# Attention and mixer on one core: tails of two pairs together, more seven-product parts, another order of loads

## The chip, the core and the metric

The kernel runs on one core of a Trainium2 chip. Its engines run side by side, each with its own queue of instructions: TensorE (PE; its weight loads are listed apart as PEld), VectorE (DVE), ScalarE (ACT), GpSimd (POOL) and SyncE (SP). POOL and SP issue most of the DMA transfers. The metric is the time of one execution in microseconds (us) on the device, the median of several runs.

## The reference

Sliding-window attention with a linear bias (window 128, 8 heads of 64), and on its output a mixer: a two-layer product over the 576 tokens, added to its input, then a two-layer product over the 512 channels with 1536 hidden units, added again.

```python
batch, n_heads, seq, head_dim = (8, 8, 576, 64)
mask = (rel >= 0) & (rel < window)
scores = np.where(mask, scale * q @ k.T + bias, -1e9)
attn = softmax(scores); x = attn @ v            # heads side by side: (8, 576, 512)
h = np.maximum(xt @ w_tok1, 0.0) @ w_tok2       # xt: x with tokens and channels exchanged
u = x + h.transpose(0, 2, 1)
h2 = np.maximum(u @ w_ch1, 0.0) @ w_ch2         # 512 -> 1536 -> 512
return u + h2
```

## The kernel before

**Tiling.** The 576 tokens of a batch are four blocks of 128 and 64 left over. Two batches make a pair; the 64 + 64 left-over rows of a pair share one block of 128 rows, the tail (`TAIL`, block 8 of a pair). Matrices are bf16, sums are float32 in PSUM, which has eight banks of 512 float32 columns.

**Stages.** For batch b, `side(b)` does the attention and the token mix, `main(b)` the channel mix. `side(b + 1)` is interleaved with `main(b)`, so that the matmuls of the one fill the gaps of the other. Batch 7's `main` has no other batch beside it.

- `scores`: for each block, `q k^T` of the 128 keys before it and of its own (L693), two instructions for the even and the odd heads after that (`Exp` on ACT, L716; the mask on DVE, L726). The first block of a batch has keys of its own kind only, yet its scores lie spread in four banks, as those of the others.
- `values`: the product with v (L760), the reciprocal and the scaling (L773, L776).
- `token_mix`: the first product over the tokens (L805 for the four blocks, L815 for the 64 rows of the tail), a ReLU, the second product (L848, L844 for the tail), and the addition of x (L866). From batch 1 on, the tail's 64 rows are copied to the other half of the partitions (`xt`, L800), so that two 64-row matmuls can run side by side in L815. The result is transposed by DMAs from SP (L874; from batch 2 on).
- `main`: twelve chunks of the first channel product, each of 4 matmuls of 512 columns (L1045) and a ReLU (L1051 on ACT, L1052 on DVE). Where `UNITS[b]` is not zero, the last units of four chunks are computed with seven half-size products instead of eight (`unit`, L967, 28 matmuls of 256 columns), with four differences of the input first (`halves`, L931), copies out (L982), additions (L991) and ReLUs (L993, L995). In the kernel before only batch 7 does this, with three units.
- `second`: the second channel product for the four blocks, with seven products instead of eight (L1240), sums before it (L1070) and evictions (L1203) in the order `PRODUCTS`. The last one of batch 7 is `last_product` (L1269, L1273).
- The tail of a pair belongs to the odd batch: three `tail_piece`s of 16 matmuls of 128 columns (L1088, ReLU L1093), then 12 matmuls of 512 columns for the second product (L1133, eviction L1140, stores L1150).

**The order.** `Plan` collects all these operations with a cost and a rank and works out, before anything is emitted, in which order each engine's queue gets them; buffers come from rings (`ps` for the banks, `ob` for six output buffers, `r2` for two hidden buffers and so on). `SEEDS` shifts the ranks a little by pseudo-random amounts, and some constants (`CASTS`, `LATE`, `TURN`, `RATES`, `EV`) are the planner's due times and rates. Where the plan has PE idle early, `spin` puts in matmuls on zeros (L1325). The loads are issued by POOL in the order of the string `LOADS`: q, k, v with the number of a block; W1, W2 and P1, T0 are the weights of the token mix and their left-over rows; A0 to A3 and B0 to B3 are quarters of the two channel weights (`WC1`, `WC2`).

```python
LOADS = ("k1 q1 k2 q2 v0 k8 q8 v1 v2 v8 v3 W1 q7 q4 k4 W2 q6 "
         "k6 A0 k7 q5 A3 k5 v7 v4 A1 v6 v5 A2 B0 T0 P1 B2 B1 B3")
```

q and k of blocks 0 and 3 come by SP and ACT ahead of these, as float32.

Of the kernel before, what the change touches and what calls it, by code (L numbers as in the profile page):

```python
# [73 lines left out]
class Plan:  # L74
# [235 lines left out]
    def emit(self, spin):  # L310
# [11 lines left out]
        for _, _, go in sorted(work, key=lambda w: w[:2]):  # L322
# [13 lines left out]
PADT = False  # L336
# [9 lines left out]
SEEDS = {0: 846071, 4: 412855, 5: 343328, 6: 901394, 7: 671959, 8: 764867, 10: 416701, 11: 351752, 12: 70309, 20: 619675, 21: 120696, 22: 577973, 23: 405716, 30: 213057, 31: 165847, 32: 71954, 40: 404590, 41: 482568, 50: 286568, 51: 611926, 60: 579527, 61: 819459, 62: 379002, 70: 640395, 71: 934419, 72: 439456, 80: 109511, 81: 910233, 82: 748762, 90: 519950, 91: 197367, 101: 150347, 102: 405724, 110: 7956, 111: 36992, 112: 363882, 120: 129293, 122: 874736, 130: 359970, 131: 803027, 140: 23914, 141: 388902, 142: 496852, 150: 220523, 151: 220010, 152: 75231, 153: 900190}  # L346
# [3 lines left out]
EV = 0.0  # L350
# [6 lines left out]
HALVED = 2  # L357
BANKS = 8
ALIKE = 0
UNITS = [0, 0, 0, 0, 0, 0, 0, 3]  # L360
# [6 lines left out]
CASTS = [5000.0, 5680.0, 7560.0, 8040.0]  # L367
PACKET = 0.813
LATE = (2400.0, 3500.0)
FETCH = 9000.0  # L370
STORE = 774.0
TURN = [(792.0, 1267.0), (1380.0, 2400.0)]
RATES = [(0.37, 0.23), (0.52, 0.35), (0.47, 0.18)]
# [4 lines left out]
LOADS = ("k1 q1 k2 q2 v0 k8 q8 v1 v2 v8 v3 W1 q7 q4 k4 W2 q6 "  # L378
         "k6 A0 k7 q5 A3 k5 v7 v4 A1 v6 v5 A2 B0 T0 P1 B2 B1 B3")
# [3 lines left out]
def kernel(  # L383
# [45 lines left out]
              lambda s: ps[:, s[0] : s[1] + 1, :].rearrange("p a b -> p (a b)"))  # L429
    ONE, TWO = [(4,), (5,), (6,), (7,)], [(0, 1), (2, 3)]  # L430
    TWICE = [(4, 5), (6, 7)]
# [9 lines left out]
    ring("v", AHEAD, [P, H, 2 * D])  # L441
# [4 lines left out]
    ring("ub", 2, [P, NB, DM])  # L446
# [4 lines left out]
    ring("uTt", 1, [P, NCB, P])  # L451
    ring("r2", 2, [P, NHT, NC * P])
    ring("r2t", 1, [P, NHT, P])
# [53 lines left out]
    for t in plan.rings["v"].slots:  # L507
        dve_.memset(t[:, :, D : D + 1], 1.0)

# [118 lines left out]
    qkT, xbs, ubs, r1s, uts, wides = {}, {}, {}, {}, {}, []  # L628
    turned, marks, turns = {}, {}, {}
# [41 lines left out]
    def scores(pr, blk, half, rank, behind=()):  # L671
# [5 lines left out]
        sp = [bank(TWO + THIRD if first else TWO) for _ in range(2)]  # L677
# [8 lines left out]
        def wide(e):  # L686
            return sp[e]().rearrange("p (i k c) -> p i k c", i=4, k=2)

        def go():
            for i in range(4):  # L690
                for kind, kb, a, z in work:
                    for e in range(2):
                        pe_.matmul(wide(e)[:, i, kind, a:z],  # L693
                                   lhsT=ts[kb]()[e * D : (e + 1) * D, NHP + i, :],
                                   rhs=ts[blk]()[e * D : (e + 1) * D, i, a:z], start=not slanted, stop=True,
                                   skip_group_check=slanted)
# [15 lines left out]

        one = pr >= MERGEM
# [20 lines left out]
    def values(pr, blk, half, pb, rank):  # L734
# [12 lines left out]
        for es in ([[0, 1]] if both else [[0], [1]]):  # L747
# [3 lines left out]
            def view(ot=ot, n=n):  # L751
                v = ot().rearrange("p (e c) -> p e c", e=n)[:, :, 0 : 4 * (D + 1)]
                return v.rearrange("p e (i d) -> p e i d", i=4)
# [35 lines left out]
    def token_mix(b, rank):  # L789
# [4 lines left out]
        pad = PADT and b > 0  # L794
# [33 lines left out]
        uTt = plan.buf("uTt") if half else None  # L828
# [3 lines left out]
        for blk in blocks:  # L832
# [29 lines left out]
            if fold:  # L862
                plan.op("ACT", 600, lambda blk=blk, ht=ht, hs=hs: act_.copy(out=ub()[:, blk, :], in_=ht()[:, hs]),
                        rk, part=(ub, blk), uses=[ht])
            else:
                plan.op("DVE", 690, lambda blk=blk, ht=ht, hs=hs: dve_.tensor_tensor(  # L866
                    out=ub()[:, blk, :], in0=ht()[:, hs], in1=xb()[:, blk, :], op=ALU.add), rk,
                    part=(ub, blk), uses=[ht], reads=tks)
        for blk in blocks:
            if b >= FROM_U:  # L870
                def turn(blk=blk):
                    c = blk % NC
                    to = uTt()[:, :, :] if blk == TAIL else uT()[:, :, c * P : (c + 1) * P]
                    nc.sync.dma_start_transpose(out=to, in_=ub()[:, blk, :])  # L874

                turned.setdefault(b, []).append(plan.op(
                    "SP", 1200, turn, rank(0), part=(uTt if blk == TAIL else uT, blk), reads=[(ub, blk)], bus=1000))
                continue
            ut = bank()

            def go(blk=blk, ut=ut):
                for cb in range(NCB):
                    pe_.transpose(ut().bitcast(BF16)[:, cb * P : (cb + 1) * P],
                                  ub()[:, blk, cb * P : (cb + 1) * P], ident[:, :])

            def copy(blk=blk, ut=ut, eng=dve_.tensor_copy):
                c = blk % NC
                to = uTt()[:, :, :] if blk == TAIL else uT()[:, :, c * P : (c + 1) * P]
                eng(out=to, in_=ut().bitcast(BF16)[:, 0 : NCB * P].rearrange("p (a b) -> p a b", a=NCB))

            rk = rank(224)
            plan.op("PE", 224, go, rk, makes=ut, reads=[(ub, blk)])
            plan.op("DVE", 425, copy, rk, part=(uTt if blk == TAIL else uT, blk), uses=[ut],
                    other=("ACT", 600, lambda copy=copy: copy(eng=act_.copy)))
        uts[b] = (uT, uTt, blocks)
# [23 lines left out]
    def halves(b, rank, uT):  # L919
# [4 lines left out]
        blks = [x for x in uts[b][2] if x != TAIL]  # L924
# [92 lines left out]
    def main(b, rank):  # L1017
        pr, half = b // 2, b % 2
        uT, uTt, blocks = uts[b]
        ub = ubs[pr]  # L1020
        r2 = plan.buf("r2")
        r2t = plan.buf("r2t") if half else None
# [58 lines left out]
        def tail_piece(t):  # L1081
            cx = bank()

            def gox(t=t, cx=cx):
                for i in range(4):
                    for cb in range(NCB):
                        tt = t - 3 + i
                        pe_.matmul(cx()[:, i * P : (i + 1) * P], lhsT=WC1[:, cb, tt * P : (tt + 1) * P],  # L1088
                                   rhs=uTt()[:, cb, :], start=cb == 0, stop=cb == NCB - 1)

            rk = rank(900)
            plan.op("PE", 896, gox, rk, makes=cx, reads=[(uTt, TAIL)], needs=[lc1[t]])
            plan.op("ACT", 600, lambda t=t, cx=cx: act_.activation(  # L1093
                out=r2t()[:, t - 3 : t + 1, :], in_=cx().rearrange("p (a b) -> p a b", a=4), func=ACT.Relu),
                rk, part=(r2t, t // 4), uses=[cx])

        if not UNITS[b]:
            turn_ = [0, 1, 2, 6, 7, 8, 3, 4, 5, 9, 10, 11] if quick else list(range(NHT))
            for at, t in enumerate(turn_):
# [3 lines left out]
                if half and at % 4 == 3:  # L1103
                    tail_piece(at)
        else:
            tt = halves(b, rank, uT)
            for u in range(NHT // 4):
# [7 lines left out]
                if half:  # L1115
                    tail_piece(4 * u + 3)
        if b == B - 1 and not quick:
            blocks = blocks[:2] + [TAIL] + blocks[2:4]
        if quick:
            second(b, rank, r2, ss, sums, ub)  # L1120
            blocks = [TAIL] if half else []
        for blk in blocks:
            cuts = [slice(0, DM)]
            if b == B - 1 and blk == blocks[-1]:
                cuts = [slice(0, DM // 2), slice(DM // 2, DM)]
            for cols in cuts:
                o2 = bank()
                n = cols.stop - cols.start
                for g in range(NHT // 3):
                    def go(blk=blk, g=g, o2=o2, cols=cols):  # L1130
                        for t in range(3 * g, 3 * g + 3):
                            l = r2t()[:, t, :] if blk == TAIL else r2()[:, t, (blk % NC) * P : (blk % NC + 1) * P]
                            pe_.matmul(o2()[:, cols], lhsT=l, rhs=WC2[:, t, cols], start=t == 0, stop=t == NHT - 1)  # L1133

                    rk = rank(648)
                    rd = [(r2t, g * 3 // 4), (r2t, (g * 3 + 2) // 4)] if blk == TAIL else [(r2, t) for t in range(3 * g, 3 * g + 3)]
                    plan.op("PE", 649 * n / DM, go, rk, reads=rd, needs=lc2[3 * g : 3 * g + 3],
                            **({"makes": o2} if g == 0 else {"adds": o2}))
                ob = plan.buf("ob")
                plan.op("DVE", 160 + 530 * n / DM, lambda blk=blk, o2=o2, ob=ob, cols=cols: dve_.tensor_tensor(  # L1140
                    out=ob()[:, cols], in0=o2()[:, cols], in1=ub()[:, blk, cols], op=ALU.add), rk, makes=ob, uses=[o2],
                    reads=[(ub, blk)])

                late = b >= FROM_P and blk not in blocks[-2:] or FROM_P <= b < B - 1
                q_ = nc.gpsimd if late else nc.sync

                def store(blk=blk, ob=ob, cols=cols, q_=q_):
                    if blk == TAIL:
                        for i in range(2):
                            (nc.scalar if i and b == B - 1 else q_).dma_start(  # L1150
                                out=out[2 * pr + i, NC * P : S, cols], in_=ob()[i * R : (i + 1) * R, cols])
                    else:
                        q_.dma_start(out=out[b, (blk % NC) * P : (blk % NC + 1) * P, cols], in_=ob()[:, cols])

                if late:
                    plan.dma(store, P, -1, uses=ob)
# [204 lines left out]
```

## Time and profile before

| | |
|---|---|
| median of 3 runs | 277.13 us (276.78 to 277.33) |
| profiled execution | 276.42 us, its span 274.7 us |
| granted TensorE clock | 0.999 |
| PE busy | 269.6 us, 2824 matmuls |
| DVE busy | 210.1 us, 496 instructions |
| ACT busy | 139.1 us, 239 instructions |
| POOL busy | 113.9 us, 144 instructions |
| moved by DMA | 38.71 MB, mean 141 GB/s |

An engine is busy while one of its instructions runs. Matmuls overlap, so the mean of one is longer than its share of the stream; the price of a matmul is read from the chain of waits, where pieces follow one another without overlap. The chain is followed back from the last instruction: at each step to what released it, or to the instruction before it on its engine.

### The profile page before, as it was taken

The page shows a single profiled execution, that of the slowest core. Times are in us where ns is not written, and L with a number is a line of the kernel's source. Part 1 is how long each engine was busy: PE and PEld are TensorE (multiplying, and loading weights), DVE is VectorE, ACT ScalarE, POOL GpSimd, SP SyncE. Part 2 cuts the span into 40 slices and gives each one's busy share as a digit, 9 for nine tenths or more (in the row PEclk, how much of TensorE's full clock was granted, in tenths as well). Part 3 has the DMA queues.
Part 4 walks back from the last instruction along what each step waited for, and adds up shares of the span by engine and source line. Part 5 has one row for each costly group of instructions (what it writes and reads, how often), then busy time and mean ns, then how long its engine had stood idle before and what let it go on. Part 6 is the DMA issues. An engine that isn't in the chain of part 4 may idle for free.

```text
span 274.7 us, 7016 instructions
## 1 busy us (share of the span) xinstructions
PE 269.6 (98%) x2824; PEld 180.3 (66%) x2824; DVE 210.1 (77%) x496; ACT 139.1 (51%) x239; POOL 113.9 (41%) x144
## 2 busy tenths in 40 slices
PE   8999999999999999999999999999999999999994
PEld 3665665676676556585658655576676745689984
DVE  7596799987897379956979468663898459966984
ACT  5475893326940388109940187106960088106660
POOL 8898747940455039700891009700453410012000
PEclk9999999999999999999999999999999999999999
DMA  8999999999999799989999759999599750044014
GB/s 155 156 165 179 179 200 182 156 146 217 115 94 135 171 215 148 155 135 203 180 143 156 186 161 89 142 153 239 73 101 132 197 128 2 2 96 155 1 41 154
DMA packets 167649, 38.71 MB, mean 141 GB/s; under 512 B 155904, under 2 KB 166784, under 8 KB 167616
## 3 DMA queue, kind: packets, MB, share of 16 engines
q0 software_dynamic: 114032, 19.77, 92.9%
q1 hardware_dynamic: 51200, 17.70, 33.1%
q10 hardware_dynamic: 2384, 0.79, 1.4%
q8 instruction: 22, 0.36, 0.5%
q14 instruction: 11, 0.09, 0.1%
HBM read 35.85 MB, written 9.44 MB: 165 GB/s over the span
## 4 chain that ended last, share of the span: by engine, by line
PE 94%; DVE 2%; DMA 2%; issue 0%
PE ps L1240 26%; PE ps L1045 25%; PE ps L760 7%; PE ps L693 7%; PE ps L805 5%; PE ps L848 5%; PE ps L1088 4%; PE ps L1133 4%; PE ps L967 3%; PE ps L1325 2%; PE ps L653 2%; DMA raw<-in_k_dram 2%; PE ps L815 1%; DVE pe L726 1%; PE ps L844 1%; PE ps L1030 1%
## 5 line engine op out<-in xcount | busy, mean ns | idle before, releaser
L1045 PE MATMUL ps<-uT,WC 128*128 128x512 bf16 x328 | 79.2, 379 | 0.0
L716 ACT ACTIVATE pe<-ps 128x1024 bf16<-128x1024 f32 (+1 forms) x76 | 63.4, 891 | 19.1 <-PE ps L693 18.7
L530 POOL DMA_DIRECT2D v<-in_v_dram x40 | 34.1, 858 | 92.0 <-PE ps L760 88.9
L1051 ACT ACTIVATE r<-ps 128x512 bf16<-128x512 f32 x77 | 45.1, 605 | 51.0 <-PE ps L1045 48.9
L1045 PEld LDWEIGHTS <-WC 128*128 128x128 bf16 x328 | 29.1, 97 | 29.0 <-issue 0.6
L726 DVE TENSOR_TENSOR pe<-pe,mask 128x1024 bf16<-128x1024 bf16 (+1 forms) x64 | 38.6, 609 | 11.7 <-ACT pe L716 11.2
L1240 PEld LDWEIGHTS <-r 128*128 128x128 bf16 x372 | 36.1, 98 | 7.3
L530 POOL DMA_DIRECT2D qk<-in_k_dram x38 | 33.1, 879 | 4.0 <-DMA WC<-in_moe_w_ch_dram 2.4
L530 POOL DMA_DIRECT2D qk<-in_q_dram x38 | 32.8, 870 | 1.7 <-PE ps L1240 0.7
L1240 PEld LDWEIGHTS <-s 128*128 128x128 bf16 x288 | 27.5, 98 | 6.0 <-issue 2.0
L776 DVE TENSOR_TENSOR xb<-ps,rt 128x256 bf16<-128x256 f32 (+1 forms) x72 | 28.9, 417 | 0.8
L760 PEld LDWEIGHTS <-pe 128*128 128x128 bf16 (+1 forms) x560 | 22.6, 98 | 9.1 <-DVE pe L726 1.3
L760 PE MATMUL ps<-v,pe 128*128 128x65 bf16 (+1 forms) x560 | 26.9, 194 | 0.2
L1240 PE MATMUL ps<-WC,r 128*128 128x256 bf16 x192 | 25.4, 273 | 0.0
L1240 PE MATMUL ps<-WT,s 128*128 128x256 bf16 x192 | 24.8, 273 | 0.0
L866 DVE TENSOR_TENSOR ub<-ps,xb 128x512 bf16<-128x512 f32 x34 | 21.3, 683 | 2.5 <-PE ps L848 2.5
L1240 PE MATMUL ps<-WT,r 128*128 128x256 bf16 x180 | 22.3, 273 | 0.0
L693 PEld LDWEIGHTS <-qkT 64*128 64x128 bf16 x560 | 14.8, 94 | 10.7 <-issue 7.8
L1203 DVE TENSOR_TENSOR raw<-ps,ub 128x512 f32<-128x512 f32 x22 | 15.0, 686 | 8.1 <-PE ps L1240 8.0
L693 PE MATMUL ps<-qkT 64*128 64x128 bf16 (+1 forms) x304 | 19.5, 216 | 0.0
L1093 ACT ACTIVATE r2t<-ps 128x512 bf16<-128x512 f32 x12 | 7.2, 600 | 22.8 <-PE ps L1088 22.4
L773 DVE RECIPROCAL rt<-ps 128x4 f32<-128x4 f32 (+1 forms) x76 | 12.6, 176 | 7.2 <-PE ps L760 6.8
(101 smaller groups left out, 347.7 us busy)
## 6 DMA issues: line engine op xcount, KB each, us to landing
v<-in_v_dram POOLq DMA_DIRECT2D x32, 128.0 KB, 5.3
qk<-in_k_dram POOLq DMA_DIRECT2D x30, 128.0 KB, 5.0
qk<-in_q_dram POOLq DMA_DIRECT2D x30, 128.0 KB, 5.0
out_dram<-raw SPq DMA_DIRECT2D x13, 256.0 KB, 2.6
WC<-in_moe_w_ch_dram POOLq DMA_DIRECT2D x8, 384.0 KB, 9.4
out_dram<-raw SPq DMA_DIRECT2D x13, 128.0 KB, 5.9
out_dram<-ob SPq DMA_DIRECT2D x4, 256.0 KB, 2.7
out_dram<-ob POOLq DMA_DIRECT2D x4, 256.0 KB, 2.7
```

The source lines that it names most:

```text
L530: nc.gpsimd.dma_start(out=to()[p0 : p0 + n, :, :], in_=rows(src, b, s0, n))
L693: pe_.matmul(wide(e)[:, i, kind, a:z], lhsT=ts[kb]()[e * D : (e + 1) * D, NHP + i, :], rhs=ts[blk]()[e * D : (e + 1) * D, i, a:z], start=n ...
L716: act_.activation(out=pb()[:, e, :, lo:, c0:c1_], in_=wide(e)[:, :, lo:, c0:c1_], func=ACT.Exp, scale=scale)
L726: dve_.tensor_tensor(out=o, in0=o, in1=heads(mk, es), op=ALU.mult)
L760: pe_.matmul(view()[a:z, at, i, :], lhsT=pb()[:, e, i, kind, a:z], rhs=vb()[:, h, 0 : D + 1], start=m == 0, stop=m == len(mms) - 1, skip_g ...
L776: dve_.tensor_tensor(out=x4(), in0=view()[r0:r1_, :, :, 0:D], in1=rt()[r0:r1_, 0:n, :, :].broadcast_to([r1_ - r0, n, 4, D]), op=ALU.mult)
L805: pe_.matmul(t1[j]()[:, :], lhsT=W1[:, c, j * P : (j + 1) * P], rhs=xb()[:, blk, :], start=c == 0, stop=False)
L866: plan.op("DVE", 690, lambda blk=blk, ht=ht, hs=hs: dve_.tensor_tensor(out=ub()[:, blk, :], in0=ht()[:, hs], in1=xb()[:, blk, :], op=ALU.a ...
L1045: pe_.matmul(ct()[:, :], lhsT=WC1[:, cb, t * P : (t + 1) * P], rhs=uT()[:, cb, :], start=cb == 0, stop=cb == NCB - 1)
L1051: plan.op("ACT", 600, lambda t=t, ct=ct: act_.activation(out=r2()[:, t, :], in_=ct()[:, :], func=ACT.Relu), rk, part=(r2, t), uses=[ct], o ...
L1203: dve_.tensor_tensor(out=v, in0=both(bk), in1=src, op=ALU.add)
L1240: pe_.matmul(of(bk, c), lhsT=l(t, c), rhs=w(t), start=first, stop=g == 1 and t == HK - 1, skip_group_check=True)
```

## The change

- The tails of two pairs (four batches) are kept and go through the channel mix together, in `main(3)` and `main(7)`: six pieces of 8 matmuls of 256 columns, then a new `tail_second` with seven products of 6 matmuls of 256 columns instead of eight, which keeps its sums in an `r2` buffer. In batch 3 it stands behind `second`, in batch 7 ahead of it.
- `UNITS` becomes `[0,0,0,1,2,1,2,3]`: seven-product units of the first channel product in batches 3 to 6 too.
- `PADT`: for pairs 2 and 3 the token mix takes the tail's 128 rows against weights padded with zeros, without the copy to `xt`.
- `LOJOINT`: a block with one kind of keys has the scores of all eight heads in two banks, one `Exp` and one mask.
- `HALVES`: the last product's second half is cut in two.
- `LOADS`, `SEEDS` and several of the planner's constants are new, so the whole order of the instructions is.

```diff
-PADT = False
+PADT = True
-EV = 0.0
+TAIL_FIRST = [False,True]
+EV = 1000.0
+LOJOINT = True
+HALVES = True
-UNITS = [0, 0, 0, 0, 0, 0, 0, 3]
+UNITS = [0,0,0,1,2,1,2,3]
...
-LOADS = ("k1 q1 k2 q2 v0 k8 q8 v1 v2 v8 v3 W1 q7 q4 k4 W2 q6 "
-         "k6 A0 k7 q5 A3 k5 v7 v4 A1 v6 v5 A2 B0 T0 P1 B2 B1 B3")
+LOADS = ("q2 T0 k2 k8 k1 q1 v2 v3 q8 v1 v0 k5 v8 W2 W1 q4 q5 "
+         "k4 q7 q6 k6 A2 A0 k7 v7 B0 A3 v4 A1 v5 B1 B2 B3 P1 v6")
...
-    ring("ub", 2, [P, NB, DM])
+    ring("ub", 2, [P, 2 * NC, DM])
+    ring("utl", 1, [P, 2, DM])
-    ring("uTt", 1, [P, NCB, P])
+    ring("uTt", 1, [P, NCB, 2 * P])
-    ring("r2t", 1, [P, NHT, P])
+    ring("r2t", 1, [P, NHT, 2 * P])
...
-        sp = [bank(TWO + THIRD if first else TWO) for _ in range(2)]
+        joint = LOJOINT and lo and not slanted
+        sp = [bank(TWO + THIRD + [(6, 7)])] if joint else [bank(TWO + THIRD if first else TWO) for _ in range(2)]
...
+        if joint:
+            def expos():
+                act_.activation(out=heads(pb(), [0, 1]), in_=sp[0]().rearrange("p (h k c) -> p h k c", h=8, k=1),
+                                func=ACT.Exp, scale=scale)
...
-        pad = PADT and b > 0
+        pad = PADT and pr >= HALVED
...
         def tail_piece(t):
+            uTt = tails_of(pr)[1]
+            for w in (t - 3, t - 1):
+                cx = bank()
+                def gox(w=w, cx=cx):
+                    for i in range(2):
+                        for cb in range(NCB):
+                            pe_.matmul(cx()[:, 2 * i * P : 2 * (i + 1) * P], lhsT=WC1[:, cb, (w + i) * P : (w + i + 1) * P],
+                                       rhs=uTt()[:, cb, :], start=cb == 0, stop=cb == NCB - 1)
...
+        if late_tail and TAIL_FIRST[pr // 2]:
+            tail_second(b, rank, r2t)
+        second(b, rank, r2, ss, sums, ub)
+        if late_tail and not TAIL_FIRST[pr // 2]:
+            tail_second(b, rank, r2t)
+
+    def tail_second(b, rank, r2t):
...
+        st = plan.buf("r2")
...
+        BANK = {1: g2, 6: g2, 7: g2, 4: g2, 2: g1, 5: g3, 3: g3}
+        AFTER = {6: 1, 7: 6, 4: 7, 3: 5}
...
+        for m in [1, 5, 6, 3, 2, 7, 4]:
+            l, w, s, tt = L[m]
+            bk = BANK[m]
+            def go(l=l, w=w, bk=bk, new=m not in AFTER):
+                for t in range(HK):
+                    pe_.matmul(bk()[:, 0:HN], lhsT=l(t), rhs=w(t), start=new and t == 0, stop=t == HK - 1,
+                               skip_group_check=True)
...
+            capt[m] = plan.op("DVE", 425, add, rk, makes=ob, uses=[bk], reads=[(utl, row)],
+                              needs=[capt[old]] if old else [])
...
+                        nc.sync.dma_start(out=out[4 * (pr // 2) + 2 * row + i, NC * P : S, :], in_=ob()[i * R : (i + 1) * R, :])
...
+            cuts = [slice(0, HN // 2), slice(HN // 2, HN)] if HALVES and c else [slice(0, HN)]
```

More of the change, by code (lines that the diff above doesn't have):

```diff
@@ L1114, in main @@
                     second_sums(u - 1, rk)
[L1115 removed]
+                if late_tail:
                     tail_piece(4 * u + 3)
[L1117 to L1156, printed above, removed]
[L1157 to L1158 removed]
```

197 lines of the change are left out of this document (137 added, 60 removed).

## The prediction

> **What bounds the kernel now.** I read the page first: the share of each engine, then the chain that ended last.
>
> ```profile
> span 274.7 us, 7016 instructions
> ...
> PE 269.6 (98%) x2824; PEld 180.3 (66%) x2824; DVE 210.1 (77%) x496; ACT 139.1 (51%) x239; POOL 113.9 (41%) x144
> ...
> PE 94%; DVE 2%; DMA 2%; issue 0%
> ```
>
> TensorE is busy for 269.6 of 274.7 us and carries 94% of the chain. An average can hide a stage with another limit, so the busy time per stretch comes next (columns: length, then PE, weight loads, DVE, ACT, POOL, the granted clock, DMA).
>
> ```profile
> 40.00:50.00 10.00, 9.96 (x71) 5.15 (x69) 9.85 (x23) 3.75 (x7) 6.92 (x8) 1.00 1.80 181
> 46.00:78.00 32.00, 32.00 (x357) 21.97 (x357) 28.44 (x68) 18.12 (x29) 15.49 (x19) 1.00 1.83 157
> 108.00:235.00 127.00, 127.00 (x1285) 81.61 (x1285) 93.92 (x207) 61.23 (x93) 44.98 (x56) 1.00 1.27 141
> 240.00:260.00 20.00, 20.00 (x204) 17.84 (x203) 15.26 (x30) 8.87 (x16) 2.88 (x4) 1.00 0.29 86
> ```
>
> The reader is to see that PE has no gap in the long stretches, and that it had none while DVE was busy for 28.44 of 32 us (89%). So from the first token mix on, the time is the sum of the matmuls in PE's stream. A matmul taken out shortens the end one for one, for as long as DVE and the transfers keep pace. Before that, in the first 23 us, PE waits for loads.
>
> **The matmul stream.** Prices come from pieces of the chain in which one line stands alone.
>
> ```profile
> 54.84 4.58 PE ps L1240 x42
> ...
> 62.46 0.89 PE ps L1088 x16
> ...
> 68.18 2.59 PE ps L1045 x12
> ...
> 88.85 1.29 PE ps L1133 x6
> ...
> 249.35 8.30 PE ps L967 x76
> ```
>
> A matmul of 512 columns takes 2.59/12 = 0.216 us, one of 256 columns 4.58/42 = 0.109 us (8.30/76 in L967, the same), one of 128 columns 0.89/16 = 0.056 us. The price goes with the columns; next to nothing is fixed.
>
> Seven-product units. UNITS gains one unit in batches 3 and 5 and two in 4 and 6: six more. A unit puts 7 products of 4 matmuls of 256 columns (28 x 0.109 = 3.06 us) in place of four chunks of 4 matmuls of 512 (16 x 0.216 = 3.45 us). Six of them: 6 x 0.395 = **-2.37 us**.
>
> Second product of the tails. Before, each of four pairs has 12 matmuls of 512 columns, 2 x 1.29 = 2.58 us (the last pair the same columns in halves); together 10.3 us. After, two pairs share seven products of 6 matmuls of 256 columns: 42 of them, which is exactly the quoted piece of 4.58 us. Twice that is 9.16 us: **-1.16 us**.
>
> First product of the tails. Before, 12 pieces of 16 x 128 columns at 0.89 us = 10.68. After, 12 pieces of 8 x 256 columns at 0.872 = 10.46: **-0.22 us**. The columns are the same; it moves from batches 1, 3, 5, 7 to 3 and 7.
>
> Token-mix tails over 128 rows (pairs 2 and 3, so batches 4 to 7).
>
> ```profile
> 109.84 1.73 PE ps L805 x8
> 111.56 0.32 PE ps L815 x2
> 111.89 1.42 PE ps L1240 x12
> ```
>
> Now two 64-row matmuls run side by side in 0.32 us, and the 12 products behind them take 1.42 where 12 x 0.109 is 1.31: the change of row tiling costs 0.11 on either side. After, two 128-row matmuls of 512 columns cost 2 x 0.216 = 0.43, with no change of tiling. 0.43 against 0.43: **0.0 us** on PE.
>
> The scores in two banks issue the same matmuls: 0.0 on PE. The halved last product splits six matmuls into twelve of 128 columns, the same columns; its gain is the final addition:
>
> ```profile
> 271.25 0.43 DVE L1273 TENSOR_TENSOR raw<-ps,ub 128x256 f32<-128x256 f32 x1 [0.23 <-PE ps L1269]
> ```
>
> After the last matmul 0.43 us of DVE remain, then the store. The same kind at 512 columns takes 0.69 (below), so 0.26 us per 256 columns, and 128 columns give 0.30: **-0.13 us**.
>
> PE and end together: -2.37 - 1.16 - 0.22 - 0.13 = **-3.88 us**.
>
> One rule of the Trainium skill speaks against this trade of long matmuls for shorter ones. "TensorE: Matmul & The Clock Gate", section "Back-to-back issue gap", puts a real stream at about 81 ns per matmul of 128 columns and 131 ns of 512, so that length is cheap and number is dear. By it, with 98 ns at 256 as an estimate between its two figures, the three parts would give +3.9, +1.1 and -6.1 us, -1.1 in all. The trace disagrees: 216, 109 and 56 ns.
>
> **What DVE gets instead.** Rows by form, the first four from 108 to 235 us, the rest of the whole run:
>
> ```profile
> L726 DVE TENSOR_TENSOR pe<-pe,mask 128x1024 bf16<-128x1024 bf16 x24 | 16.3, 683 | 0.2 <-ACT pe L716 0.2
> ...
> L1052 DVE TENSOR_SCALAR r<-ps 128x512 bf16<-128x512 f32 x6 | 4.1, 688 | 2.6 <-PE ps L1045 1.8 <-ACT pe L716 0.8
> ...
> L726 DVE TENSOR_TENSOR pe<-pe,mask 128x512 bf16<-128x512 bf16 x8 | 3.4, 425 | 7.1 <-ACT pe L716 6.9
> ...
> L800 DVE COPY xt<-xb 64x512 bf16<-64x512 bf16 x4 | 1.6, 410 | 0.1
> ```
>
> ```profile
> L1070 DVE TENSOR_TENSOR s<-s,r 128x768 bf16<-128x768 bf16 x16 | 8.8, 552 | 0.1
> ...
> L991 DVE TENSOR_TENSOR r<-ps,raw 128x512 bf16<-128x512 f32 x6 | 4.1, 688 | 1.6 <-ACT raw L982 1.5
> ...
> L993 DVE TENSOR_SCALAR r<-r 128x512 bf16<-128x512 bf16 x6 | 1.7, 290 | 0.1
> ...
> L1140 DVE TENSOR_TENSOR raw<-ps,ub 128x512 f32<-128x512 f32 x2 | 1.4, 692 | 1.2 <-PE ps L1133 1.2
> ...
> L931 DVE TENSOR_TENSOR tt<-uT,tt 128x512 bf16<-128x512 bf16 x2 | 0.8, 424 | 0.1
> ```
>
> All six units lie in that stretch. Added there: in each of four batches four differences at 0.424 (6.8 us); per unit three additions at 0.688 (12.4 us) and about two of three ReLUs at 0.29, as now in batch 7, where 6 of 9 are on DVE (3.5 us); for the tails four sums at 0.55 and seven evictions at 0.43, less two at 0.69 (3.8 us). Taken away: four copies at 0.41 (1.6 us), four merged masks at 2 x 0.425 - 0.683 (0.7 us), and the ReLUs of L1052 (4.1 us), for which ACT has room at 61 of 127 us, since 24 chunks fewer need one. DVE goes from 93.9 to 93.9 + 26.5 - 6.4 = 114.0 us. PE goes from 127 to about 124 us there (2.37 and the tails' share less). DVE is at 92%.
>
> Does PE then wait? The nearest rows are 46 to 78 us, 89% with no gap, and 40 to 50 us, 9.85 of 10 with 0.04 us of gap. The cost lies between nothing and 4.1 us (the rival below); I take **+0.3 us**, nearest to the two rows. A gain is excluded, since PE has no gap there to close.
>
> New waits: in each tail's seven products, product 4 follows product 7 in the same bank and waits for its eviction. PE takes matmuls in order, so everything behind it stands too, unless the written order puts other matmuls between. Cover: chunks of batch 4 for the first tail, the last batch's own second product for the second. I cost it at nothing; with the cover gone it is an eviction of 0.43 us and the way there and back (L1273 began 0.23 us after PE was done), 0.7 us for each tail, 1.4 in all, which the range holds.
>
> Buffers and queues: the tail sums take one of the two r2 buffers, free once the batch's second product is done and wanted again one batch later; the rows held for two pairs are read out a good part of a batch before the next pair writes them. The tail's four stores go to SP, ahead of transposes:
>
> ```profile
> 158.10 1.16 SPq L1150 DMA_DIRECT2D out_dram<-ob  x2
> 159.43 1.29 SPq L642 DMA_TRANSPOSE qkT<-qk  x1
> ```
>
> Each takes 0.58 us of SP, so a transpose behind all four starts 2.3 us later and its scores with it; the chunks of the running batch, which wait for none of these transposes, cover that. I cost it at nothing; without the cover it is up to 2.3 us, once. Two stores fewer lie on POOL's queue among the loads.
>
> **The start.** The order of the loads is new, and loads land one after another. Timeline of the POOL issues, then the time to landing of each of them:
>
> ```profile
> 13.42 0.78 POOL L534 DMA_DIRECT2D W<-in_moe_w_tok_dram  x1
> ...
> 16.57 0.88 POOL L530 DMA_DIRECT2D qk<-in_k_dram  x1
> 17.43 0.72 POOL L534 DMA_DIRECT2D W<-in_moe_w_tok_dram  x1
> ...
> 19.89 0.80 POOL L534 DMA_DIRECT2D WC<-in_moe_w_ch_dram  x1
> ```
>
> ```profile
> W<-in_moe_w_tok_dram POOLq DMA_DIRECT2D x1, 256.0 KB, 5.3
> qk<-in_k_dram POOLq DMA_DIRECT2D x1, 128.0 KB, 4.9
> WC<-in_moe_w_ch_dram POOLq DMA_DIRECT2D x1, 384.0 KB, 7.0
> ```
>
> ```profile
> GB/s 155 156 165 179 179 200 182 156 146 217 115 94 135 171 215 148 155 135 203 180 143 156 186 161 89 142 153 239 73 101 132 197 128 2 2 96 155 1 41 154
> ```
>
> W1 lands at 18.7, k4 at 21.5, W2 at 22.7, the first quarter of WC1 at 26.9. So W2 took about 1.3 us behind k4; a block of 128 KB takes about 0.85 at the 155 GB/s of the page's first slices (the last fence). PE, for this:
>
> ```profile
> 19.57 0.59 PE L805 MATMUL ps<-xb,W 128*128 128x512 bf16 x2
> ...
> 21.64 0.60 PE L815 MATMUL ps<-xb,W1p 64*128 64x512 bf16 x2
> ...
> 22.97 0.59 PE L848 MATMUL ps<-r,W 128*128 128x512 bf16 x2
> ```
>
> The new order puts T0 (32 KB, 0.2), k5 (0.85) and W2 (1.3) ahead of W1: W1 lands 2.4 us later, at 21.1. It had 0.9 us of slack before L805. Then L805 (1.73) and L815 (0.54) run without the gaps they have now, to 23.4; L848 follows 0.73 behind L815's end as now, at 24.2 instead of 22.97: **+1.2 us**. The first quarter of WC1 to land is A2, 1.9 us later than A0 now (T0, k5 and q5 are more ahead of it), A0 another 1.9 us behind it. Three chunks on A2 fill that time. Bounds: 0, if PE does in those 1.2 us transposes that it would do later anyway, and +3.8, if everything waits for A0. No input of the first token mix comes earlier, so a gain is excluded.
>
> **Sum:** -3.88 + 0.3 + 1.2 = -2.4 us. The profiled execution took 276.42 us (its span and 1.7 us around it) and would go to 274.0; it lies 0.7 under the median of 277.13, so the median goes to **274.7 us**. A measurement of this kernel tells about 0.2%, 0.55 us, from no change.
>
> **The rivals.**
> DVE becomes the bound (slower). Place: 108 to 235 us. If DVE can't be kept busier than the 89% seen over a long stretch, 114.0 us of it take 128.1 us where PE needs 124: +4.1 for the 0.3. It decides from 110 us of DVE work on in that stretch. Time: 277.13 - 3.88 + 1.2 + 4.1 = 278.5. For it: my count lies above that point. Against it: 40 to 50 us, and that the ReLUs can go to ACT.
> The start waits for A0. +3.8 for +1.2: 277.3, no change. Against it: A2's chunks and batch 1's attention need no A0.
> The start costs nothing. 273.5. For it: PE fills its gaps in the start with empty matmuls, so work could be drawn forward.
> Matmuls cost by number, not by columns. The three parts change the count by +72, +24 and -96: no gain on PE, 277.13 - 0.13 + 1.2 + 0.3 = 278.5. It is the mechanism behind the skill's rule above; the three prices speak plainly against it.
>
> **How the numbers follow.** Forecast 0.55 (its own range 273.7 to 276.3), start free 0.17, start waits for A0 0.10, DVE bound 0.17, price by number 0.01. Faster: 0.55 + 0.17 = 0.72. Same: 0.06 of the A0 case and 0.02 of a mild DVE case, 0.08. Slower: the rest, 0.20. The range goes from 0.6 below the free start, 272.9, to the DVE case, 278.6; above it lie DVE cases with more work left on that engine.
>
> **What would show it.** L967 with 84 + 168 = 252 matmuls and L1045 with 96 fewer, at the same prices; DVE near 234 us in all (210.1, the 20.1 above, 3.8 for the second tail) with PE still without gaps between 108 and 235 us; L848's first matmul near 24.2 us; the tails' products in 4.6 us per two pairs. Waits of PE for DVE of over 1 us in that stretch, or L848 after 26 us, would make the prediction wrong.

## The result and the profile after

| | before | after |
|---|---|---|
| median, 9 runs of each | 277.04 us (276.48 to 278.12) | 275.40 us (275.07 to 276.44) |
| ratio of the two | | 0.9945 (0.9925 to 0.9964) |
| profiled execution | 276.42 us, span 274.7 | 275.81 us, span 273.7 |

The changed kernel is faster by 1.6 us (0.6%). The forecast was 2.4 us, to 274.7; the measured median lies 0.7 above it and inside the range.

In the code, each line of before has moved. The names stay: chunks L1087, unit L1008 (its additions L1032), tail products L1131 and L1220 (evictions L1235), second product L1328 (evictions L1291), token mix L849, L859 and L891, `xt` copy L844, last product L1360 with its additions L1364, empty matmuls L1420.

The page of the changed kernel: span, engines, chain.

```profile
span 273.7 us, 7090 instructions
...
PE 264.7 (97%) x2803; PEld 188.5 (69%) x2832; DVE 230.1 (84%) x545; ACT 147.6 (54%) x257; POOL 113.2 (41%) x142
...
PE 88%; DVE 7%; DMA 2%; issue 1%; DVEq 0%; SPq 0%
```

PE is still the bound. Two things must be read with care. There are 2832 weight loads and only 2803 matmuls: 29 records of matmuls are missing, so PE's busy time and its gaps can't be read off directly, and I count by weight loads where that matters. And DVE now holds 7% of the chain (4% in a second profile), where it held 2%.

The same stretches as before (the columns are PE, weight loads, DVE, ACT, POOL, clock, DMA):

```profile
40.00:50.00 10.00, 8.59 (x132) 6.92 (x131) 9.61 (x28) 4.30 (x11) 6.21 (x8) 1.00 1.90 177
46.00:78.00 32.00, 30.22 (x339) 19.22 (x343) 29.75 (x77) 19.18 (x34) 18.18 (x23) 1.00 1.90 161
108.00:235.00 127.00, 125.68 (x1328) 91.46 (x1343) 111.85 (x247) 69.60 (x113) 41.41 (x51) 1.00 1.21 139
```

From 108 to 235 us DVE has 111.85 us of work (114.0 were forecast); 15 matmul records are missing there, and 15 of at most 0.22 us are more than the 1.3 us in which PE seems idle. The stretch that did not keep its form is 40 to 50 us: PE was busy for 9.96, now for 8.59, with no record missing. The waits of PE name the place:

```profile
PE ps L681 <- DVE xb L820: 1.4, 1, 1.4
PE ps L1420 <- DVE zero L499: 1.0, 1, 1.0
PE ps L804 <- DVE pe L769: 0.5, 1, 0.5
PE ps L1087 <- DMA uT<-ub: 0.4, 1, 0.4
```

The second of these stands at the very start and was there before. The first is new: one wait of 1.4 us for DVE. It is at 48 us, as the timelines of PE and then of DVE show:

```profile
47.44 0.82 PE L1328 MATMUL ps<-WC,r 128*128 128x256 bf16 x6
49.66 0.61 PE L681 MATMUL ps<-ident,qk 128*128 128x128 bf16 x8 [1.41 <-DVE xb L820]
```

```profile
46.14 0.56 DVE L598 TENSOR_TENSOR WT<-WC 128x768 bf16<-128x768 bf16 x1
46.71 0.68 DVE L844 COPY xt<-xb 64x512 bf16<-64x512 bf16 x1
47.40 1.03 DVE L598 TENSOR_TENSOR WT<-WC,WT 128x768 bf16<-128x768 bf16 x2
48.46 0.18 DVE L817 RECIPROCAL rt<-ps 128x4 f32<-128x4 f32 x1
48.56 0.53 DVE L1112 TENSOR_TENSOR r<-r 128x768 bf16<-128x768 bf16 x1
49.01 0.31 DVE L817 RECIPROCAL rt<-ps 128x4 f32<-128x4 f32 x3
49.24 1.06 DVE L820 TENSOR_TENSOR xb<-ps,rt 128x256 bf16<-128x256 f32 x3
```

DVE runs without a pause here. The scalings (L820) free the banks that the transposes of L681 want. They stand in DVE's queue behind three weight sums of L598, whose inputs are the late quarters of the second channel weight, and behind a copy to `xt` (L844) that took 0.68 us, where such a copy mostly takes 0.29 (the last section says when it doesn't).

### The profile page after: what moved, and what is told of

Its sections match the earlier page's. It is cut to its first block, busy times and chain, and to the rows that moved or that the text cites. A ratio compares the mean times of both kernels' runs of the same rounds, so it can differ in the third digit from the quotient of the medians.

```text
span 273.7 us, 7090 instructions
## 1 busy us (share of the span) xinstructions
PE 264.7 (97%) x2803; PEld 188.5 (69%) x2832; DVE 230.1 (84%) x545; ACT 147.6 (54%) x257; POOL 113.2 (41%) x142
## 4 chain that ended last, share of the span: by engine, by line
PE 88%; DVE 7%; DMA 2%; issue 1%; DVEq 0%; SPq 0%
PE ps L1328 22%; PE ps L1087 18%; PE ps L1008 10%; PE ps L724 6%; PE ps L804 6%; PE ps L849 5%; PE ps L891 4%; PE ps L1131 4%; PE ps L1420 3%; PE ps L1220 3%; DMA uT<-ub 2%; PE ps L681 2%; DVE WT L598 1%; PE ps L859 1%; DVE ub L909 1%
## 5 line engine op out<-in xcount | busy, mean ns | idle before, releaser
L759 ACT ACTIVATE pe<-ps 128x1024 bf16<-128x1024 f32 (+1 forms) x62 | 56.0, 957 | 18.9 <-PE ps L724 18.5
L1087 PE MATMUL ps<-uT,WC 128*128 128x512 bf16 x214 | 55.2, 379 | 1.5 <-DMA uT<-ub 0.4
L1093 ACT ACTIVATE r<-ps 128x512 bf16<-128x512 f32 x53 | 31.1, 603 | 21.3 <-PE ps L1087 21.0
L1328 PEld LDWEIGHTS <-r 128*128 128x128 bf16 x372 | 35.6, 98 | 6.1 <-issue 0.6
L1087 PEld LDWEIGHTS <-WC 128*128 128x128 bf16 x232 | 20.6, 98 | 20.5 <-issue 0.8
L769 DVE TENSOR_TENSOR pe<-pe,mask 128x1024 bf16<-128x1024 bf16 (+1 forms) x50 | 32.6, 661 | 0.5 <-ACT pe L759 0.2
L1328 PEld LDWEIGHTS <-s 128*128 128x128 bf16 x288 | 27.8, 98 | 4.0 <-issue 0.2
L820 DVE TENSOR_TENSOR xb<-ps,rt 128x256 bf16<-128x256 f32 (+1 forms) x68 | 27.5, 417 | 0.8
L804 PEld LDWEIGHTS <-pe 128*128 128x128 bf16 (+1 forms) x560 | 22.2, 98 | 7.0 <-DVE pe L769 1.3
L804 PE MATMUL ps<-v,pe 128*128 128x65 bf16 (+1 forms) x560 | 25.9, 194 | 0.5 <-DVE pe L769 0.5
L1328 PE MATMUL ps<-WC,r 128*128 128x256 bf16 x192 | 25.1, 273 | 0.1
L1328 PE MATMUL ps<-WT,s 128*128 128x256 bf16 x192 | 24.4, 273 | 0.0
L1328 PE MATMUL ps<-WT,r 128*128 128x256 bf16 x180 | 22.1, 273 | 0.0
L909 DVE TENSOR_TENSOR ub<-ps,xb 128x512 bf16<-128x512 f32 x30 | 19.1, 683 | 1.1 <-PE ps L891 0.9
L746 ACT ACTIVATE pe<-ps 128x1024 bf16<-128x1024 f32 x7 | 7.2, 1023 | 23.1 <-PE ps L724 23.1
L1291 DVE TENSOR_TENSOR raw<-ps,ub 128x512 f32<-128x512 f32 x23 | 15.7, 686 | 3.3 <-PE ps L1328 3.2
L849 PE MATMUL ps<-xb,W 128*128 128x512 bf16 x57 | 15.8, 379 | 0.4
```

What stands on the lines that cost most here:

```text
L759: act_.activation(out=pb()[:, e, :, lo:, c0:c1_], in_=wide(e)[:, :, lo:, c0:c1_], func=ACT.Exp, scale=scale)
L769: dve_.tensor_tensor(out=o, in0=o, in1=heads(mk, es), op=ALU.mult)
L804: pe_.matmul(view()[a:z, at, i, :], lhsT=pb()[:, e, i, kind, a:z], rhs=vb()[:, h, 0 : D + 1], start=m == 0, stop=m == len(mms) - 1, skip_g ...
L820: dve_.tensor_tensor(out=x4(), in0=view()[r0:r1_, :, :, 0:D], in1=rt()[r0:r1_, 0:n, :, :].broadcast_to([r1_ - r0, n, 4, D]), op=ALU.mult)
L849: pe_.matmul(t1[j]()[:, :], lhsT=W1[:, c, j * P : (j + 1) * P], rhs=xb()[:, blk, :], start=c == 0, stop=False)
L909: plan.op("DVE", 690, lambda blk=blk, u=u_of(pr, blk)[1], ht=ht, hs=hs: dve_.tensor_tensor(out=u(), in0=ht()[:, hs], in1=xb()[:, blk, :], ...
```

## The experiments

**Theory:** the time is the sum of the matmuls in PE's stream, priced by their columns, plus what the new order of loads costs the start. **Rivals:** DVE, now fuller, sets the time from 108 us on; the start costs nothing or much more; the order itself decides, whatever the work.

The twelve runs came in four groups, each on another chip, and each group has its own runs of the kernel before beside it (medians 276.83, 276.79, 276.76 and 277.22). Ratios are to those, and each can differ a little from the quotient of the two medians. Between groups it is safer to compare how far each lies under its own kernel before: 1.6 us in the result above.

### The changed kernel again

> The changed kernel once more, beside the next three on one chip, as their base. Both theories: 275.4 us, 1.6 us under the kernel before.

275.32 us, ratio 0.9954 (0.9937 to 0.9970): 1.5 us faster. In this profile the wait of L681 is 1.0 us instead of 1.4, since the copy ahead of it takes 0.29 instead of 0.68, and the wait of L1087 for the transfer of `uT` is gone. It is what the others are compared with.

### Twelve matmuls more

```diff
+                if b in (4, 5):
+                    pe_.matmul(ct()[:, :], lhsT=WC1[:, 0, t * P : (t + 1) * P], rhs=uT()[:, 0, :],
+                               start=True, stop=True)
```

Twelve chunks issue their first matmul twice; the order is kept.

> The changed kernel with the first matmul of each of the 12 chunks of batches 4 and 5 issued twice: 12 x 0.216 = 2.6 us more on PE, the order of every queue as it is. Theory 1 (from the first token mix on the time is PE's stream, and DVE at 88% between 108 and 235 us still keeps pace): +2.6 us, 278.0. Rival (DVE at 88% has become the limit of that stretch): PE has slack there and takes most of it up, under +1 us, 276.2 at most.

277.97 us, ratio 1.0049 (1.0031 to 1.0067), so 2.65 us above the changed kernel. Twelve times 0.216 us is 2.6. A matmul of 512 columns costs its stream price at the end, one for one. That is the theory's first part.

### DVE made fuller, in the changed kernel and in the one before

```diff
+    def more():
+        for _ in range(3):
+            dve_.memset(idle[:, :], 0.0)
...
-    plan.emit(spin)
+    plan.emit(spin, [(t, -2, more) for t in [110e3 + 10e3 * k for k in range(12)]])
```

Nobody waits for these 36 memsets.

> The changed kernel with three empty DVE memsets (about 0.17 us each) every 10 us from 110 to 220 us, about 6 us of DVE in all, the order otherwise as it is. Theory 1: DVE's gaps take them up, under +0.7 us, 275.4 to 276.1. Rival (DVE is the limit there): +4 to +6 us, 279.5 to 281.5.

> The kernel before with the same 36 empty DVE memsets between 110 and 220 us (6 us of DVE). If it is DVE's fullness (88% in the changed kernel, 74% in this one) that made them cost 1.7 us there: 0 to +0.4 us here, 276.8 to 277.2. If any insertion into DVE's queue delays what PE wants next: +1.5 to 2 us here too, 278.3 to 278.8.

In the changed kernel: 277.03 us, ratio 1.0014 (1.0002 to 1.0026), 1.7 us more. In the kernel before: 278.52 us, ratio 1.0057 (1.0036 to 1.0078), 1.7 us more. Groups of DVE, then the stretch of 108 to 235 us, for the changed kernel with the memsets:

```profile
L1428 DVE MEMSET idle<- 128x128 uint32 x36 | 5.9, 165 | 2.2
...
108.00:235.00 127.00, 125.11 (x1315) 90.29 (x1330) 113.38 (x280) 69.59 (x113) 41.06 (x51) 1.00 1.24 137
```

and for the kernel before with them:

```profile
108.00:235.00 127.00, 126.36 (x1271) 80.78 (x1270) 96.90 (x240) 60.32 (x93) 45.92 (x57) 1.00 1.31 142
```

The memsets take 5.9 us by their own durations. Part of that overlaps with their neighbours: DVE's busy time grows by 3.1 us (230.0 to 233.1) in the changed kernel and by 4.4 (210.1 to 214.5) in the one before. They cost 1.7 us where DVE is busy for 113.38 of 127 us, and the same 1.7 where it is busy for 96.90. If fullness were what costs, the second would have cost less. So DVE's load isn't a bound at 89% either.

The traces say what costs. The order of PE is the same with and without the memsets, so the profiles can be laid side by side, weight load by weight load. Between 108 and 225 us the changed kernel falls behind by 2.1 us (against its second profile), the kernel before by 1.6. Both do so in a few steps of 0.1 to 0.5 us, most of them within 2 us behind one of the twelve places; five of the twelve cost nothing in the one, seven in the other. Where PE's pauses show at these steps, they are for DVE (0.35 us at 113, 0.19 at 184). So what costs is that a piece put in at some places delays the one result that PE wants next. The first run alone would have been read as a DVE bound in part; the second one decides.

### W1 loaded earlier

```diff
+    names = LOADS.split()
+    at = plan.items[names.index("k5")][0].t0
+    for i, o in enumerate(plan.items[names.index("W1")]):
+        o.t0 = at - 10 + i
```

> The changed kernel with the transfer of W1 sent ahead of k5, v8 and W2, the order of all else as it is: W1 lands about 2.6 us earlier, v8 and W2 about 1.3 us later. Theory 1a (W1's landing at 21.1 us sets the start): L891 starts near 23.2 instead of 24.4 us and the end comes 1.2 us earlier, 274.2. Rival 1b (the queue of loads as a whole sets it: the first quarter of WC1 lands at 28.4 us whatever lies before it): PE is earlier at L891 but waits for A2 or, later, on DVE, and gains 0.3 us or nothing, 275.1 to 275.4.

275.73 us, ratio 0.9963 (0.9950 to 0.9976): no gain. Timeline of PE:

```profile
19.55 0.42 PE L804 MATMUL ps<-v,pe 128*128 128x65 bf16 x8 [0.52 <-DVE pe L769]
19.81 0.78 PE L1420 MATMUL ps<-zero 128*128 128x484 bf16 x3
20.44 0.82 PE L804 MATMUL ps<-v,pe 128*128 128x65 bf16 x16
21.10 0.58 PE L1420 MATMUL ps<-zero 128*128 128x496 bf16 x2
21.52 1.89 PE L849 MATMUL ps<-xb,W 128*128 128x512 bf16 x7
```

L849 starts no earlier (21.15 and 21.59 us in the two profiles of the changed kernel), although its weight landed at 18.1 us instead of 21.1: in PE's order the values (L804) and empty matmuls (L1420) sized for the planned landing still stand ahead of it. With the order kept, an earlier load can't show its worth. The run says nothing about the start, except that W1's landing alone no longer sets it once the order is written.

### The old order of loads

```diff
...
-LOADS = ("q2 T0 k2 k8 k1 q1 v2 v3 q8 v1 v0 k5 v8 W2 W1 q4 q5 "
-         "k4 q7 q6 k6 A2 A0 k7 v7 B0 A3 v4 A1 v5 B1 B2 B3 P1 v6")
+LOADS = ("k1 q1 k2 q2 v0 k8 q8 v1 v2 v8 v3 W1 q7 q4 k4 W2 q6 "
+         "k6 A0 k7 q5 A3 k5 v7 v4 A1 v6 v5 A2 B0 T0 P1 B2 B1 B3")
```

All else as after. The seeds of the order were found anew: in the first run for all batches, in the second only for the first ones, so that the late order stayed nearly that of after (and there the copy of batch 1 was planned with the 0.68 us of the first profile).

> The changed kernel with LOADS as before and with seeds found anew for that. Theory 1 (the new order of loads costs 1.4 us at the start and brings the wait of 1.0 to 1.4 us on DVE near 48 us): the second product's first matmul near 23.0 us instead of 24.4, no wait of over 0.5 us near 48, 275.3 - 2.0 = 273.3. Rival (the loads come soon enough either way; what PE lacks at first it does later): 275.0 to 275.6.

> The changed kernel with LOADS as before, and new seeds for the first batches alone, so that PE's order after 100 us is nearly the same as in the changed kernel (in loads_back it was another). Theory 1 (the new order of loads costs 0.9 to 2 us in the first 60 us): 273.4 to 274.4, PE without the wait near 48 us. Rival (loads_back was no faster, so the order of loads gives nothing; PE waits elsewhere instead): 275.0 to 276.8.

276.82 us, ratio 1.0003 (0.9982 to 1.0024), and 276.78 us, ratio 1.0001 (0.9984 to 1.0018). Both are slower than the changed kernel by about 1.5 us, where the theory wanted them faster. The start does what it should; PE's timeline in the first of the two:

```profile
23.74 0.60 PE L891 MATMUL ps<-r,W 128*128 128x512 bf16 x2 [0.19 <-DMA W<-in_moe_w_tok_dram]
```

That is 0.7 us earlier than after (24.42, below; 23.39 in the second run), and neither has a wait near 48 us. But the waits of PE in the second are:

```profile
PE ps L724 <- DMA qkT<-qk: 1.2, 1, 1.2
...
PE ps L1087 <- DVE xb L820: 0.7, 2, 0.4
PE ps L1087 <- DMA uT<-ub: 0.6, 1, 0.6
```

What the start gives is paid later: 1.2 us for a transpose at 92 us, 0.7 and 0.6 elsewhere. In the first run it goes into small pauses around 95, 104, 213 and 241 us. So the earlier start was real, and it wasn't worth its 1.2 us at the end. Whether an order exists that keeps both stays open: I had two orders of the old loads, not the best one.

### The units taken back, and the units alone

```diff
-UNITS = [0,0,0,1,2,1,2,3]
+UNITS = [0, 0, 0, 0, 0, 0, 0, 3]
```

in the changed kernel, with the seeds of the order found anew; and the opposite edit in the kernel before, with its seeds as they were.

> The changed kernel with UNITS as before (seven-product units in batch 7 alone) and with seeds found anew for that, so that PE's order has no planned waits. Theory 1 (the six units are worth what they take off PE, 2.4 us, less little): 275.3 + 2.1 = 277.4. Rival (the 20 us that they put on DVE eat most of it): 275.3 to 276.2.

> The kernel before with nothing but the new UNITS; its seeds were found for the old ones. If columns on PE decide whatever the order: 277 - 2.4 = 274.6. If the order written for each queue decides (DVE's and the output buffers' turns no longer meet PE's): waits of several us in batches 4 to 6, 290 us or more.

Without the six units: 277.14 us, ratio 1.0006 (0.9991 to 1.0020). By this they are worth 1.8 us where the sum had 2.37, and the rest of the change together nets nothing. But the order is another too, and its start is worse: the second product begins at 25.16 us (24.42 after), behind a wait that the changed kernel has for 0.5 us only,

```profile
PE ps L804 <- DVE pe L769: 1.2, 1, 1.2
```

while its wait at 48 us is only 0.2. So the 1.8 us are the units and two orders together, not a clean price of the units. The units alone: 305.0 us, ratio 1.1014 (1.0969 to 1.1059), slower by 28 us with less work on PE. Its waits:

```profile
PE ps L1088 <- DMA uTt<-ub: 7.5, 1, 7.5
PE ps L1045 <- DMA uT<-ub: 5.9, 1, 5.9
```

Orders that were fitted to the old work put matmuls ahead of transposes that come late for them. The new work pays only with an order of its own: "new order" is as much part of this change as the products.

### The last product in one piece, and one copy fewer

```diff
-HALVES = True
+HALVES = False
```

> The changed kernel with the last product's second half in one piece again (HALVES off), the order otherwise as it is. As the prediction had it (a shorter last addition): +0.13 us. Rival (the two halves cost more than they save: from the last matmul to the end the span holds 3.6 us in the kernel before and 3.9 in the changed one): -0.25 us.

274.96 us, ratio 0.9928 (0.9910 to 0.9946), 0.36 us under the changed kernel's 275.32; the two intervals just overlap. The end of the timeline, after and then without the halves:

```profile
268.54 1.49 PE L1360 MATMUL ps<-WT,r 128*128 128x256 bf16 x18
268.07 0.58 DVE L1412 MEMSET zero<- 128x1 bf16 x5
268.73 0.44 DVE L1413 MEMSET zero<- 128x1 bf16 x4
269.21 0.69 DVE L1291 TENSOR_TENSOR raw<-ps,raw 128x512 f32<-128x512 f32 x1
...
269.82 0.41 DVE L1364 TENSOR_TENSOR ob<-ps,ub 128x256 f32<-128x256 f32 x1
270.15 0.48 DVE L1364 TENSOR_TENSOR raw<-ps,ub 128x128 f32<-128x128 f32 x2
```

```profile
267.80 1.47 PE L1360 MATMUL ps<-WT,r 128*128 128x256 bf16 x12
269.08 0.41 DVE L1364 TENSOR_TENSOR ob<-ps,ub 128x256 f32<-128x256 f32 x1
269.41 0.42 DVE L1364 TENSOR_TENSOR raw<-ps,ub 128x256 f32<-128x256 f32 x1
```

From PE's end (270.03; 269.27) to the end of the last addition are 0.60 us with halves and 0.56 without. The halves gain nothing: two additions of 128 columns take 0.48, one of 256 takes 0.42, and they can't start when their matmuls are done, because DVE is behind here. From 267.43 us on the chain runs through DVE: an eviction, ten small memsets (L1412, L1413), the last eviction (L1291), the additions. The one at 269.82 starts 0.46 us after its last matmul. In the kernel before, DVE had waited 0.23 us for PE ahead of each of the last two additions.

The 0.36 us aren't the edit's by these traces. Up to the last product the kernel issues the same instructions in the same order as the changed one; laid beside the latter's second profile, it is ahead by 0.30 us at 21.6 us already, and by 0.34 at the end. That is a difference of two executions at the start.

```diff
-            plan.op("DVE", 395, lambda: dve_.tensor_copy(out=xt()[far, :], in_=xb()[own, TAIL, :]), rank(0),
+            plan.op("DVE", 395, lambda: b == 1 or dve_.tensor_copy(out=xt()[far, :], in_=xb()[own, TAIL, :]), rank(0),
...
-                rs, rhs = (far, xt()[far, :]) if xt and j else (own, xb()[own, TAIL, :])
+                rs, rhs = (far, xt()[far, :]) if xt and j and b != 1 else (own, xb()[own, TAIL, :])
```

Batch 1's copy at 46.71 us is not issued, and its two 64-row matmuls run one after the other; the order is kept.

> The changed kernel with batch 1's two 64-row matmuls of the tail one after the other, without the copy to the other partitions; the order as it is. The copy takes 0.68 us of DVE at 46.7 us, ahead of the scalings that PE waits for near 48; PE gets 0.22 us more. Theory 1c (DVE's queue from 41 to 49 us is what PE waits for): the wait falls from 1.2 to about 0.6 us, the end comes 0.4 us earlier, 274.9. Rival (that stretch waits for the last loads, the quarters of WC2 or v6, and the copy only fills the time): 0 to +0.2 us, 275.3 to 275.5.

274.87 us, ratio 0.9924 (0.9906 to 0.9943), 0.45 us under the changed kernel; again the two intervals just overlap. The waits of PE, but for the one at the very start:

```profile
PE ps L681 <- ACT xb L826: 0.6, 1, 0.6
```

With the copy gone from DVE's queue, the wait at 48 us falls from 1.0 (1.4 in the first profile) to 0.6, and the releaser is no longer DVE but ACT's scaling. So that wait is DVE's queue, and it is on the path. How much of the 0.45 us is the copy's is less sure. Beside the second profile of the changed kernel, PE is ahead by 0.28 us at 21.6 us, where nothing differs yet, by 0.59 behind the wait, by 0.40 once the two matmuls have run one after the other, and by 0.71 at the end. So the edit's own part is 0.3 us of wait less 0.2 us of matmuls; the rest came at the start and near 247 us.

> The changed kernel with HALVES off and without the copy of batch 1 (the edits of no_halves and no_xt1 together), the order otherwise as it is. If the two gains (0.36 and 0.45 us) lie at places of PE's stream that do not touch, they add: 275.3 - 0.8 = 274.5, about 0.990 of the kernel before. Rival (a wait further on takes up what the first stretch gives): 274.9.

Both edits together: 275.32 us, ratio 0.9938 (0.9919 to 0.9956). The two gains didn't add. In this group the kernel before took 277.22, so this run lies 1.9 us under it, as the one without the copy does (1.9) and the one without halves (1.8). The wait at 48 us is 0.6 here too. Beside the run without the copy, this profile loses 0.3 us at 29 us, where a chunk waits for a quarter of WC1, and 0.4 at 213 us, where one waits for `uT` (as in the first profile of the changed kernel): places that neither edit touches. A few tenths between two kernels that differ only slightly in their order are not to be put down to one edit. The lowest median is that without batch 1's copy, 274.87; the three lie within each other's intervals.

## Why the prediction was right

**Prices and columns of PE: right.** Groups of the changed kernel, then pieces of its chain:

```profile
L1008 PE MATMUL ps<-tt,WS 128*128 128x256 bf16 x108 | 15.7, 272 | 0.1
L1008 PE MATMUL ps<-uT,WC 128*128 128x256 bf16 x72 | 10.6, 272 | 0.0
L1008 PE MATMUL ps<-uT,WS 128*128 128x256 bf16 x36 | 5.4, 273 | 0.1
L1008 PE MATMUL ps<-tt,WC 128*128 128x256 bf16 x36 | 5.4, 272 | 0.1
L1087 PEld LDWEIGHTS <-WC 128*128 128x128 bf16 x232 | 20.6, 98 | 20.5 <-issue 0.8 <-DMA WC<-in_moe_w_ch_dram 0.3
```

```profile
62.46 2.59 PE ps L1087 x12
118.13 0.87 PE ps L1131 x8
154.33 2.62 PE ps L1220 x24
243.24 3.96 PE ps L1008 x36
```

The unit has 108 + 72 + 36 + 36 = 252 matmuls, as forecast; the chunks have 232 (by weight loads), 96 fewer. The prices stand: 2.59/12 = 0.216 at 512 columns, 2.62/24 = 0.109 and 3.96/36 = 0.110 at 256, and a tail's piece of 8 takes 0.87. Forty-two of L1220 are 4.6 us per two pairs. Priced in this way, and with the empty matmuls of L1420 left out, all matmuls of the kernel come to 247.7 us before and 243.9 after: 3.8 less, where the parts on PE had said 3.75. The rival by number of matmuls, and with it the rule in "TensorE: Matmul & The Clock Gate" of the Trainium skill, section "Back-to-back issue gap", falls by the same rows and by the run with twelve matmuls more.

**But they didn't all arrive at the end.** PE's last matmul ended 1.2 us earlier, not 3.8, in these two executions (which differ by 0.6 us, where the medians differ by 1.6). Empty matmuls grew by 0.46 us (7.55 to 8.01), and what is then left of the time up to the last matmul, in which PE does nothing, grew by 2.2 us (15.8 to 18.0; 1.9 in the second profile). The next points say where.

**The start, +1.2: right.** Timeline of PE after:

```profile
21.15 1.90 PE L849 MATMUL ps<-xb,W 128*128 128x512 bf16 x7
22.98 0.60 PE L859 MATMUL ps<-xb,W1p 64*128 64x512 bf16 x2
24.42 1.03 PE L891 MATMUL ps<-r,W 128*128 128x512 bf16 x4
```

L849 starts behind W1 at 21.15 (21.1 forecast) and L891 at 24.42 (24.2 forecast, 22.97 before). Counted by the same prices, PE has by 24 us lost 1.2 us more than in the kernel before (1.6 in the second profile). What the prediction didn't see is that this figure can't be had back by the loads alone: the two runs with the old loads started earlier and ended later.

**The wait at 48 us: missed.** This is the step that failed. The prediction took the row of 40 to 50 us, DVE busy for 9.85 of 10 with no gap in PE, as a sign that DVE that full costs PE nothing, and used it for the stretch from 108 us on. It didn't ask what the change does to that row itself. There the new order puts weight sums, a copy and the scalings into a queue with no slack, and 1.0 to 1.4 us of PE are lost; taking the copy out shortened the wait to 0.6. It is enough for what the forecast lacked (0.7 of 2.4 us), though I haven't shown that it is the whole of it.

**DVE from 108 to 235 us, +0.3: too much.** The work was well counted (111.85 of 114.0), and no wait of PE for DVE of over 0.2 us is left there. The memsets show that the load as such has no price that could be told from that of the places.

**The tails, the joint scores and the wider token mix: not seen at the end.** The columns came off as forecast: without the six units the sum of matmuls is 246.3 us, so 1.4 of the 3.8 us are the tails'. But that kernel takes the time of before, 277.14 against 276.79, where the prediction's terms without the units and DVE (-1.16 - 0.22 - 0.13 + 1.2) give -0.3. In its own order the tails' gain goes into the start, where its second product begins 2.2 us later than in the kernel before, and into 0.5 us at 105 us. No run has the tails alone, so their price at the end stays open. The new waits that the prediction priced at nothing (product 4 behind 7's eviction, the stores on SP) don't appear among PE's waits.

**The halves, -0.13: wrong.** The end gained nothing by them (0.60 us with, 0.56 without). The step that failed took the duration of one addition of 128 columns (0.30 estimated, 0.28 in the trace) for the time from PE's end to DVE's end. That supposes that DVE waits for PE there, as it did in the kernel before; in the new order DVE is the one that is behind, and both halves queue up behind the 256-column addition.

## What to carry to other kernels

Where one engine's stream is the bound, price a change by that engine's own stream price and check the sum against the stream, not only against the time: here 3.8 us left the stream and 1.6 reached the end. Then look in the old profile for the places where a second engine has no slack, and ask of each of them what the change puts into that queue. Load on an engine that isn't the bound has no price by its percentage (the same 36 instructions cost 1.7 us at 76% and at 89%); its price is the delay of the one result that the bound engine wants next. And so a hand-fitted order must be fitted again for new work: the units alone, in the old order, cost 28 us.

## What the hardware showed that was not expected

The copy to `xt`, 64x512 bf16, takes 0.29 us or up to 0.76, by what POOL does. Timeline of POOL in the first profile of the changed kernel (DVE's copy at 46.71, 0.68 us, stands above):

```profile
46.43 0.88 POOL L537 DMA_DIRECT2D v<-in_v_dram  x1 [1.80 <-DMA WC<-in_moe_w_ch_dram]
```

Timeline of both engines in the second profile of the same kernel:

```profile
47.20 0.88 POOL L537 DMA_DIRECT2D qk<-in_q_dram  x1
47.26 0.29 DVE L844 COPY xt<-xb 64x512 bf16<-64x512 bf16 x1
```

In the first the copy starts 0.28 us into the issuing of a load, and ends just behind it: 46.71 + 0.68 = 47.39, the issue 46.43 + 0.88 = 47.31. In the second it starts 0.06 us into one and isn't held. The fourteen profiles hold 52 such copies. Seventeen of them started between 0.24 and 0.58 us into an issue, and each ended 0.08 to 0.12 us after that issue's end. The other 35, with no issue beside them or started in its first 0.23 us or its last 0.2, took 0.29 to 0.30 us. So for the later part of an issue POOL keeps DVE's copy out. The Trainium skill, "SBUF — State Buffer", section "SBUF: two separate sides", has a pair of ports that these two engines lock against each other: the one that starts first has it for its whole instruction, and the other waits. The rows agree in that the copy waits for the issue's end; they differ from "the whole instruction" in that a copy that starts in the first 0.23 us of an issue isn't held. The additions and subtractions of two inputs (L1112) are not held: all 64 took 0.53 to 0.56 us, the 11 that started in that later part of an issue too. This is where the wait at 48 us gets its spread of 0.4 us between two profiles.

And 29 matmuls of 512 columns left no record in two profiles of the same kernel while all their weight loads did, so a gap in PE of 0.21 us in such a trace may be no gap. The run without batch 1's copy, which issues as many, has 2832 records of both.
